# Low halves of the split operands 64 bytes off in SBUF, and the order of three matmuls

## The chip, the core and the metric

The kernel runs on one core of one Trainium2 chip. The metric is the device time of one execution in microseconds (us). Engines are called by the profile's names: PE (TensorE matmul), PEld (TensorE weight load), DVE (VectorE), ACT (ScalarE), POOL (GpSimd) and SP (the queue that issues the DMAs here).

## What is computed

The reference chains three parts over 2 x 576 = 1152 tokens of 512 features:

```python
scores = where(mask, q @ k.T / 8, -1e9); x = softmax(scores) @ v      # 8 heads of 64; a window of 32, or 32 with dilation 4
h = x @ w_in; x = (h * tanh(softplus(h))) @ w_out                     # 512 -> 2048 -> 512, called the first layer here
out = sum_e p[:, e] * (relu(x @ w1[e]) @ w2[e])                       # 4 experts, 512 -> 1024 -> 512, p normalised over e
```

All inputs and outputs are float32.

## The kernel before

**Split operands.** Nearly every large product is made three times. A float32 value is split into a high part (rounded to the type that the kernel calls float32r, by ACT) and a low part (the rest, by DVE or POOL), and a product x·y is taken as high·high + high·low + low·high, three matmuls into one PSUM bank. The tiles come in pairs: `xh`/`xl` (activations), `wxh`/`wxl` (weights of the first layer's units 0 to 3, later other operands), `gh`/`gl` (outputs of the activation function), and `late0`/`late1` and `late2`/`late3` (weights of the other units, later the experts' weights). Each tile is one block per partition; all slices that the matmuls read are whole multiples of 128 bytes long and begin at multiples of 128 bytes inside their tile. Before the change each of these ten tiles begins at a multiple of 128 bytes of its partition: their sizes are multiples of 128 bytes, and the tile `pad` of 48 floats stands behind the three `raw` tiles, `prob` and `psum_e`, whose sizes are not.

**A matmul and its load.** A matmul reads a stationary operand of 128 columns, which a weight load brings into the array, and streams a moving operand of N columns (N is 256, 320 or 512 here, 4 bytes a column and partition) past it. While one matmul streams, the load for the next one runs.

**The four places with split products.** Line 566 (`Step1.first`, x @ w_in), line 590 (`Step1.second`, the activated values @ w_out), line 786 (`Group.prod`, an expert's first products, as seven block products of a Strassen form) and line 861 (`Group.second`, an expert's second products). Their orders of the three matmuls, as (stationary, moving):

- line 566: (w high, x high), (w high, x low), (w low, x high)
- line 590: (w high, g high), (w low, g high), (w high, g low)
- line 786: (a high, b high), (a high, b low), (a low, b high)
- line 861: (g high, w high), (g high, w low), (g low, w high)

**Stages.** Attention runs to about 64 us, with the first steps of the first layer between its pieces. The first layer runs to about 256 us: 48 visits of a unit (16 units for each of three groups of 512, 320 and 320 tokens), each with 12 matmuls of line 566 and 12 of line 590. `steps[i].first()` is issued before `steps[i - 1].second()`, so that ACT and DVE (lines 574 and 575, `split`) make `gh`/`gl` of a step while PE does another. Step 0 takes its low activations last (`lo_last`). Then 4 experts x 2 token sets x 4 pairs of feature blocks run as 32 groups: 42 matmuls of line 786 in each (7 products x 6), and of line 861 24 (set 0, N = 256 in line 786) or 30 (set 1, N = 320). The last group takes its last row in two halves, which makes 6 matmuls more. So there are 576 + 576 + 1344 + 870 = 3366 split matmuls out of 4152; the others belong to attention. Each engine executes in the order written. Nothing waits for an output before the end except the store of the result.

Of the kernel before, what the change touches and what calls it, by code (L numbers as in the profile page):

```python
# [8 lines left out]
F32 = mybir.dt.float32  # L9
F32R = mybir.dt.float32r  # L10
# [13 lines left out]
def kernel(  # L24
# [18 lines left out]
    NT = B * S  # L43
# [3 lines left out]
    NUA = 4  # L47
# [5 lines left out]
    SETS = ((0, 256), (512, 320))  # L53
    GW = 640
    PW = 2816
    EXP, MISH = "exp_and_friends", "mish"

    big = ctx.enter_context(tc.tile_pool(name="big", bufs=1))
# [8 lines left out]
    def bank(n):  # L67
        return ps.tile([128, 512], F32, tag=f"bank{n}", name=nm("bank"))
# [2 lines left out]

    xh = big.tile([128, 4 * NT], F32R, name="xh")
    xl = big.tile([128, 4 * NT], F32R, name="xl")

    wxh = big.tile([128, 1024 * NUA], F32R, name="wxh")
    wxl = big.tile([128, 1024 * NUA], F32R, name="wxl")

    gh = big.tile([128, 2 * GW], F32R, name="gh")  # L80
    gl = big.tile([128, 2 * GW], F32R, name="gl")
    raws = [big.tile([128, 4104], U8, name=f"raw{n}") for n in range(3)]
    prob = big.tile([128, NT // 128, NE], F32, name="prob")
    psum_e = big.tile([128, NT // 128], F32, name="psum_e")
    big.tile([128, 48], F32, name="pad")

    scr = big.tile([128, NT // 128 * DM], F32, name="scr")
    hbuf = [scr[:, GW * n:GW * (n + 1)] for n in (0, 1)]
# [19 lines left out]
    late = []  # L108
# [436 lines left out]
    class Step1:  # L545
# [27 lines left out]
        def split(self):  # L573
            ACT.activation(self.ghi, self.hc, AF.Copy)  # L574
            DVE.tensor_tensor(out=self.glo, in0=self.hc, in1=self.ghi.bitcast(F32), op=ALU.subtract)  # L575

        def second(self, lo_last=False, units_at=(0, 1)):
            if self.grp not in yacc:
                yacc[self.grp] = [bank(b)[:, 0:self.w] for b in ((0, 1, 2, 3), (4, 5, 0, 1), (2, 3, 4, 5))[self.grp]]
            for i, u in enumerate(self.us):  # L580
                if i not in units_at:
                    continue
                wh, wl = units[u]
                g = slice(self.w * i, self.w * (i + 1))
                order = [(d, k) for d in range(4) for k in range(3)]
                if lo_last:
                    order.sort(key=lambda o: o[1] == 2)
                for d, k in order:
                    a, x = ((wh, self.ghi), (wl, self.ghi), (wh, self.glo))[k]
                    PE.matmul(yacc[self.grp][d], a[:, 512 + 128 * d:640 + 128 * d], x[:, g],  # L590
                              start=u == UORD[self.grp][0] and k == 0, stop=u == UORD[self.grp][-1] and k == 2)

# [12 lines left out]
    for n in (0, 1):  # L605
        o = 2 * GW * (n + 1)
# [114 lines left out]
    def prep_a(n):  # L721
        o = PW * (n % NP2)
        r = stage1.rearrange("p (c f m) -> p c f m", c=4, f=2)
        a12 = [w[:, o:o + 512].rearrange("p (c m) -> p c m", c=4) for w in late[2:4]]
        a22 = [w[:, o + 512:o + 768].rearrange("p (c m) -> p c m", c=2) for w in late[2:4]]
        split(*a12, r[:, :, 0], DVE)
        split(*a22, r[:, 2:4, 1], DVE)
        a11, a12, a21, a22 = blocks()
        POOL.tensor_tensor(out=a22, in0=a21, in1=a22, op=ALU.add)  # L729
        POOL.tensor_tensor(out=a21, in0=a11, in1=a21, op=ALU.subtract)  # L730
        POOL.tensor_tensor(out=a11, in0=a22, in1=a11, op=ALU.subtract)
        POOL.tensor_tensor(out=a12, in0=a12, in1=a11, op=ALU.subtract)

    def prep_s(n):
        o = PW * (n % NP2) + 768
        split(late[2][:, o:o + 1024], late[3][:, o:o + 1024], stage1, DVE)
        load_w1(n + 1)
        ready.add(("s", n))

    def w2_hi(n):  # L740
        o = PW * (n % NP2) + 1792
        ACT.activation(late[2][:, o:o + 1024], stage2, AF.Copy)  # L742

    def w2_lo(n):
        o = PW * (n % NP2) + 1792
        hi, lo = (t[:, o:o + 1024] for t in late[2:4])
        POOL.tensor_tensor(out=lo, in0=stage2, in1=hi.bitcast(F32), op=ALU.subtract)  # L747
        load_w2(n + 1)
        ready.add(("w2", n))
# [5 lines left out]
    def amat(name, p, k):  # L755

        o = PW * p
        o += {"A11": 128 * k, "A12": 256 + 128 * k, "A22": 512 + 128 * k, "S2": 768 + 256 * k, "S3": 896 + 256 * k,
# [3 lines left out]
    class Group:  # L762
# [90 lines left out]
        def second(self, f, which=slice(None)):  # L853
            assert ("w2", self.e * NP2 + self.p) in ready
            o = PW * self.p + 1792 + 512 * f
            wh, wl = (w[:, o:o + 512] for w in late[2:4])
# [103 lines left out]
    u1.x_lo()  # L960
    att.close()
    wpb = ctx.enter_context(tc.tile_pool(name="wpb", bufs=1))
    late += [wpb.tile([128, n], F32R, name=f"late{i}") for i, n in enumerate((1024, 1024, 11264, 11264))]
    late.append(wpb.tile([128, 640], F32, name="late4"))


# [28 lines left out]
    for e in range(1, NE):  # L995
        for p in range(NP2):
            n, g = e * NP2 + p, 2 * NP2 * (e - 1) + NP2 + p + 1
# [67 lines left out]
```

## Time and profile before

| | |
|---|---|
| median of 3 runs | 632.99 us (632.98 to 633.09) |
| profiled execution, its own time | 635.62 us |
| its span, first to last instruction | 633.8 us |
| mean granted TensorE clock | 0.997 |
| PE busy | 625.5 us (99%), 4152 matmuls |
| PEld busy | 562.2 us (89%), 4152 loads |
| DVE, ACT, POOL busy | 287.0, 261.9, 180.5 us |

A matmul's recorded duration is longer than the distance to the next one, because matmuls are pipelined. Busy time counts overlapping matmuls once. What a matmul costs in a row of them is the distance from start to start, called the pitch below: the length of a piece in the chain that ended last divided by its count, or the difference of two starts in the timeline.

### The profile page before, as it was taken

How to read it: one execution, taken by the hardware profiler on the slowest of the kernel's cores; microseconds unless marked ns; L12 is line 12 of the kernel's file. 1: busy time of each engine (PE TensorE's matmuls, PEld its weight loads, DVE VectorE, ACT ScalarE, POOL GpSimd, SP SyncE). 2: the span in 40 equal slices, each digit the busy share in tenths (PEclk: the TensorE clock that was granted, in tenths of full speed). 3: DMA queues.
4: the chain of work that ended last, by engine and by line, in shares of the span. 5: the costliest groups of instructions: out<-in, count | busy, mean ns of one | idle time of the engine just before them, and what ended most of it. 6: DMA issues, size and time to landing. Idle time of an engine off the chain costs nothing.

```text
span 633.8 us, 10146 instructions
## 1 busy us (share of the span) xinstructions
PE 625.5 (99%) x4152; PEld 562.2 (89%) x4152; DVE 287.0 (45%) x482; ACT 261.9 (41%) x497; POOL 180.5 (28%) x201
## 2 busy tenths in 40 slices
PE   8998999999999999999999999999999999999997
PEld 5776888889999999998998899998999988989986
DVE  6887677613111333474534523444523444424223
ACT  7786777624223443452344322444322443322220
POOL 8763555512100242180243200234200335100000
PEclk9998999999999999999999999999999999999999
DMA  8865677300000122020023200123100132000102
GB/s 192 195 184 156 222 223 220 128 1 1 1 1 1 67 79 87 1 101 1 13 88 100 66 1 1 34 78 90 67 1 0 34 101 66 2 1 30 38 1 83
DMA packets 51358, 43.66 MB, mean 69 GB/s; under 512 B 26352, under 2 KB 44144, under 8 KB 51312
## 3 DMA queue, kind: packets, MB, share of 16 engines
q1 hardware_dynamic: 51312, 43.02, 22.9%
q8 instruction: 32, 0.52, 0.3%
q14 instruction: 14, 0.11, 0.1%
HBM read 40.65 MB, written 2.36 MB: 68 GB/s over the span
## 4 chain that ended last, share of the span: by engine, by line
PE 92%; DMA 3%; DVE 2%; SPq 1%; ACT 1%; POOL 0%; issue 0%; DVEq 0%; POOLq 0%
PE bank L861 31%; PE bank L786 28%; PE bank L590 16%; PE bank L566 15%; DMA raw<-in_moe_w_out_dram 1%; DMA scr<-in_moe_w_in_dram 1%; DMA vP<-in_v_dram 1%; DMA natk<-in_k_dram 1%; DVE pr L383 1%; DVE mx L382 1%; PE bank L326 0%; SPq L282 0%; PE bank L396 0%; ACT pr L384 0%; PE bank L374 0%; POOL vP L289 0%
## 5 line engine op out<-in xcount | busy, mean ns | idle before, releaser
L786 PE MATMUL bank<-xh,late 128*128 128x256 f32 (+1 forms) x512 | 120.4, 296 | 0.0
L786 PE MATMUL bank<-wxh,late 128*128 128x320 f32 (+1 forms) x384 | 94.9, 296 | 0.0
L786 PEld LDWEIGHTS bank<-xh,late 128*128 128x128 f32 x512 | 89.1, 190 | 1.8
L861 PE MATMUL bank<-late,gh 128*128 128x512 f32 x280 | 87.0, 392 | 0.0
L729 POOL TENSOR_TENSOR raw<-raw 128x256 f32<-128x256 f32 x16 | 12.2, 764 | 225.1 <-DVE late L618 225.1
L566 PE MATMUL bank<-xh,late 128*128 128x320 f32 (+1 forms) x288 | 75.9, 336 | 0.0
L786 PE MATMUL bank<-xl,late 128*128 128x256 f32 (+1 forms) x256 | 75.7, 296 | 0.0
L590 PE MATMUL bank<-gh,late 128*128 128x320 f32 (+1 forms) x288 | 72.0, 336 | 0.0
L786 PEld LDWEIGHTS bank<-wxh,late 128*128 128x128 f32 x384 | 68.5, 190 | 0.6
L575 DVE TENSOR_TENSOR gl<-scr,gh 128x512 fp32r<-128x512 f32 (+1 forms) x32 | 24.5, 767 | 80.0 <-ACT gh L574 80.0
L861 PEld LDWEIGHTS bank<-late,gh 128*128 128x128 f32 x280 | 50.9, 188 | 9.0
L571 ACT ACTIVATE scr<-bank 128x320 f32<-128x320 f32 (+1 forms) x48 | 23.5, 489 | 83.4 <-PE bank L566 83.4
L747 POOL TENSOR_TENSOR late<-raw,late 128x1024 fp32r<-128x1024 f32 x16 | 38.8, 2422 | 64.8 <-ACT late L742 64.8
L786 PE MATMUL bank<-wxl,late 128*128 128x256 f32 (+1 forms) x192 | 56.9, 296 | 0.1
L861 PE MATMUL bank<-late,gl 128*128 128x512 f32 x140 | 54.5, 389 | 0.0
L566 PEld LDWEIGHTS bank<-xh,late 128*128 128x128 f32 x288 | 50.6, 188 | 3.8
L590 PEld LDWEIGHTS bank<-gh,late 128*128 128x128 f32 x288 | 50.1, 188 | 3.7
L861 PE MATMUL bank<-late,late 128*128 128x512 f32 (+1 forms) x219 | 52.8, 388 | 0.0
L786 PEld LDWEIGHTS bank<-xl,late 128*128 128x128 f32 x256 | 48.5, 190 | 1.8
L566 PE MATMUL bank<-xl,late 128*128 128x320 f32 (+1 forms) x144 | 48.3, 336 | 0.0
L590 PE MATMUL bank<-gl,late 128*128 128x320 f32 (+1 forms) x144 | 48.3, 336 | 0.0
L861 PE MATMUL bank<-late,wxh 128*128 128x512 f32 (+1 forms) x154 | 47.4, 389 | 0.0
(153 smaller groups left out, 1137.3 us busy)
## 6 DMA issues: line engine op xcount, KB each, us to landing
raw<-in_moe_w_dram SPq DMA_DIRECT2D x32, 512.0 KB, 3.4
raw<-in_moe_w_out_dram SPq DMA_DIRECT2D x15, 512.0 KB, 3.6
raw<-in_moe_w_in_dram SPq DMA_DIRECT2D x9, 512.0 KB, 4.2
scr<-in_moe_w_in_dram SPq DMA_DIRECT2D x7, 512.0 KB, 4.9
natk<-in_k_dram SPq DMA_DIRECT2D x8, 256.0 KB, 3.5
natq<-in_q_dram SPq DMA_DIRECT2D x8, 256.0 KB, 4.0
out_dram<-scr SPq DMA_DIRECT2D x8, 256.0 KB, 2.0
vD<-in_v_dram SPq DMA_DIRECT2D x16, 64.0 KB, 4.1
```

The lines of the kernel that those rows point to most:

```text
L382: DVE.tensor_reduce(out=mx, in_=sv, axis=AX.X, op=ALU.max)
L383: DVE.tensor_tensor(out=self.pr, in0=sv, in1=mx.unsqueeze(2).to_broadcast([128, 8, 64]), op=ALU.subtract)
L566: PE.matmul(h, a[:, c, :], x[:, c, :], start=c == 0 and k == 0, stop=c == 3 and k == 2)
L571: ACT.activation(self.hc[:, self.w * i:self.w * (i + 1)], h, AF.Mish)
L575: DVE.tensor_tensor(out=self.glo, in0=self.hc, in1=self.ghi.bitcast(F32), op=ALU.subtract)
L590: PE.matmul(yacc[self.grp][d], a[:, 512 + 128 * d:640 + 128 * d], x[:, g], start=u == UORD[self.grp][0] and k == 0, stop=u == UORD[self.gr ...
L729: POOL.tensor_tensor(out=a22, in0=a21, in1=a22, op=ALU.add)
L747: POOL.tensor_tensor(out=lo, in0=stage2, in1=hi.bitcast(F32), op=ALU.subtract)
L786: PE.matmul(out, w, x(k), start=first and k == 0 and i == 0, stop=k == 1 and i == 2, skip_group_check=not first)
L861: PE.matmul(acc, x[:, s], a[:, cols], start=self.p == 0 and f == 0 and i == 0, stop=self.p == NP2 - 1 and f == 1 and i == 2, skip_group_ch ...
```

## The change

The low tiles get 32 floats more, and their slice begins 16 floats (64 bytes) inside; the pad shrinks to 16 floats. In line 590 the second and third matmul change places.

```diff
+    LINE = 16
...
+    def lo_tile(pool, n, name):
+        return pool.tile([128, n + 2 * LINE], F32R, name=name)[:, LINE:LINE + n]
+
     xh = big.tile([128, 4 * NT], F32R, name="xh")
-    xl = big.tile([128, 4 * NT], F32R, name="xl")
+    xl = lo_tile(big, 4 * NT, "xl")
 
     wxh = big.tile([128, 1024 * NUA], F32R, name="wxh")
-    wxl = big.tile([128, 1024 * NUA], F32R, name="wxl")
+    wxl = lo_tile(big, 1024 * NUA, "wxl")
 
     gh = big.tile([128, 2 * GW], F32R, name="gh")
-    gl = big.tile([128, 2 * GW], F32R, name="gl")
+    gl = lo_tile(big, 2 * GW, "gl")
...
-    big.tile([128, 48], F32, name="pad")
+    big.tile([128, 16], F32, name="pad")
...
                 if lo_last:
-                    order.sort(key=lambda o: o[1] == 2)
+                    order.sort(key=lambda o: o[1] == 1)
                 for d, k in order:
-                    a, x = ((wh, self.ghi), (wl, self.ghi), (wh, self.glo))[k]
+                    a, x = ((wh, self.ghi), (wh, self.glo), (wl, self.ghi))[k]
...
-    late += [wpb.tile([128, n], F32R, name=f"late{i}") for i, n in enumerate((1024, 1024, 11264, 11264))]
+    for i, n in ((0, 1024), (2, 4 * PW)):
+        late += [wpb.tile([128, n], F32R, name=f"late{i}"), lo_tile(wpb, n, f"late{i + 1}")]
```

## Rows read from the trace of the kernel before

**Rows 1.** The page, parts 1 and 4: busy time, and the chain that ended last.

```profile
span 633.8 us, 10146 instructions
PE 625.5 (99%) x4152; PEld 562.2 (89%) x4152; DVE 287.0 (45%) x482; ACT 261.9 (41%) x497; POOL 180.5 (28%) x201
...
PE 92%; DMA 3%; DVE 2%; SPq 1%; ACT 1%; POOL 0%; issue 0%; DVEq 0%; POOLq 0%
```

**Rows 2.** Stretches: window in us, PE busy (matmuls), other engines, PEclk, DMA share, GB/s.

```profile
44.00:72.00 28.00, 25.71 (x180) 19.65 (x179) 19.96 (x39) 19.42 (x32) 12.41 (x12) 0.94 0.57 173
72.00:140.00 68.00, 68.00 (x306) 56.62 (x306) 42.47 (x58) 42.79 (x72) 33.31 (x24) 1.00 0.49 155
140.00:250.00 110.00, 110.00 (x746) 109.51 (x745) 30.96 (x41) 39.75 (x71) 19.95 (x18) 1.00 0.09 29
384.00:478.00 94.00, 94.00 (x554) 85.20 (x553) 39.28 (x69) 32.41 (x64) 21.50 (x20) 1.00 0.15 46
```

**Rows 3.** Chain that ended last, in pieces: start us, length us, what, matmuls.

```profile
11.09 0.44 PE bank L326 x4
...
89.21 2.72 PE bank L566 x12
91.93 2.72 PE bank L590 x12
...
147.94 3.52 PE bank L590 x24
151.47 3.52 PE bank L566 x24
...
352.27 4.31 PE bank L786 x36
...
396.19 4.39 PE bank L786 x30
400.58 3.42 PE bank L861 x15
```

**Rows 4.** Timeline at a change from N = 512 to N = 256: start us, length us, instruction.

```profile
340.72 0.39 PE L861 MATMUL bank<-late,gl 128*128 128x512 f32 x1
...
340.95 0.28 PE L786 MATMUL bank<-xh,late 128*128 128x256 f32 x1
340.95 0.19 PEld L786 LDWEIGHTS bank<-xl,late 128*128 128x128 f32 x1
...
341.06 0.28 PE L786 MATMUL bank<-xl,late 128*128 128x256 f32 x1
341.07 0.31 PEld L786 LDWEIGHTS bank<-xh,late 128*128 128x128 f32 x2
...
341.18 0.40 PE L786 MATMUL bank<-xh,late 128*128 128x256 f32 x2
341.30 0.19 PEld L786 LDWEIGHTS bank<-xl,late 128*128 128x128 f32 x1
```

**Rows 5.** Timeline of PE alone at a change from N = 320 to N = 512.

```profile
400.42 0.63 PE L861 MATMUL bank<-late,gh 128*128 128x512 f32 x2
400.89 0.39 PE L861 MATMUL bank<-late,gl 128*128 128x512 f32 x1
401.12 0.63 PE L861 MATMUL bank<-late,gh 128*128 128x512 f32 x2
401.58 0.39 PE L861 MATMUL bank<-late,gl 128*128 128x512 f32 x1
...
402.94 0.39 PE L861 MATMUL bank<-late,gl 128*128 128x512 f32 x1
```

**Rows 6.** Timeline around the second products of one step: the split, then line 590.

```profile
90.12 0.68 DVE L575 TENSOR_TENSOR gl<-scr,gh 128x512 fp32r<-128x512 f32 x1
...
91.77 0.62 PE L590 MATMUL bank<-gh,late 128*128 128x512 f32 x2
...
92.22 0.39 PE L590 MATMUL bank<-gl,late 128*128 128x512 f32 x1
```

**Rows 7.** The end of the kernel in the chain: start us, length us, what.

```profile
619.92 10.31 PE bank L861 x51
630.23 0.03 issue
630.26 0.48 DVE scr L875
```

## The prediction

> **What bounds the kernel.** I read the page's busy times and the chain that ended last first: PE is busy for 625.5 of 633.8 us, and PE makes up 92% of the chain [rows 1]. An average over stages can mislead, so the stretches come next: from 72 us on PE is busy for the whole of each stretch shown, at a granted clock of 1.00, its higher level of 2.4 GHz, while DVE, ACT and POOL are busy for well under two thirds of the same time [rows 2]. So the time is a count of matmuls times their pitch, and only something that changes the pitch can change it. The third view is the chain in pieces, which gives the pitch. Line 590 takes 2.72 us for 12 matmuls of 512 columns, 226.7 ns each, and line 566 the same, although their orders of the three products differ; 24 of 320 columns take 3.52 us, 146.7 ns each, again on both lines; 36 of 256 columns on line 786 take 4.31 us, 119.7 ns each [rows 3]. From 512 to 320 columns the pitch falls by 80.0 ns for 192 columns, 0.4167 ns a column, which is the higher clock. The streams alone then take 213.3, 133.3 and 106.7 ns, and each pitch is 13.3 ns (13.0 for the last) above that. **The gap** is the same for all three sizes and lines, and it is the time in which a stream reads 32 columns, 128 bytes of a partition. 3366 gaps of 13.3 ns are 44.8 us. [...]
>
> **The change, part by part.**
>
> *Offsets.* No instruction is added or removed: 4152 matmuls and as many loads stay. What changes is where a low operand begins: 64 bytes behind a multiple of 128. The high parts keep their place modulo 128: each low tile grows by 128 bytes, and pad goes from 192 to 64 bytes, down by 128. With each tile rounded up to 32 bytes, the three raw tiles (4128 each), prob (160) and psum_e (64) are 12608 bytes; with 64 more that is 99 times 128, as it was 100 times before.
>
> After the change the moving operands of three successive products begin at 0, 64 and 0, and the next triple at 0 again. The loads follow: the load for the next product starts with the running matmul (340.95 and 340.95, 341.06 and 341.07 [rows 4]), and with the new order on line 590 it is always the load of a high part beside a high stream and of a low part beside a low one. Load and stream thus begin at the same place modulo 128 in every pair, as they do before.
>
> No row shows an operand at 64 beside one at 0 in a split product, so the cost of the offset is bounded. [...] Above: where a row of 512 columns follows shorter ones, the first five pitches are 400.42 to 401.58, 232 ns each, and then 401.58 to 402.94, 227 ns each [rows 5]; single ones, from 400.89 to 401.12, are 230. A gap 5.3 ns longer on all would be 17.8 us more; a whole further period of 13.3 ns on the two products in three that have a low operand would be 2244 x 13.3 = 29.9 us more.
>
> I take a value between. The gap equals one period of 128 bytes at three sizes of stream, so I read it as a start that must fall on the same place of a period: a stream of a whole number of periods ends on such a place, is too late for it, and the next start waits a full period. A gap of half that length does occur: when 256 columns follow 512, the first pitch is 0.11 us (340.95 to 341.06) and the next 0.12 [rows 4]; 0.11 leaves about half of the usual gap, though with equal offsets. If a start at 64 has its place half a period later, the gaps from 0 to 64 and from 64 to 0 become 6.67 ns, and the third, from 0 to 0, stays 13.3. That is 2 x 6.67 ns off every three products: 2244 x 6.67 ns = 15.0 us. Some 60 of the products lie before 64 us, between pieces of attention and loads, where PE is idle for part of the time (25.7 us busy of 28.0 from 44 to 72 us [rows 2]); I count their 40 gaps as nothing gained, 0.3 us.
>
> *Line 590's order.* The low activations are read second instead of third, one product (147 to 227 ns) earlier, and the low weights as much later. The split that makes the low activations ends at 90.80 us here, and the first product with them starts at 92.22; in the new order it would at about 92.00 [rows 6]. Of the 32 steps this is the one with the smallest lead, and 1.2 us of it are left. So this costs nothing; without that lead, each of 31 steps (step 0 keeps its low activations last) could lose up to 0.2 us, 7 us in all. For the pitch the order by itself is worth nothing with equal offsets: lines 566 and 590 have the same one [rows 3]. It matters only with the offset, for the pairing above.
>
> *What hides a faster PE's next limit.* The other engines have over a third of each stretch free [rows 2], so they follow a PE that is 2% faster. Behind the last matmul, what remains is 0.5 us of DVE and the store [rows 7], untouched.
>
> *Sum.* The profiled execution takes 635.62 us, 2.63 above the median of 632.99; taking 14.7 us off gives 620.9 for such an execution and 618.3 for the median.
>
> **Rivals.**
>
> *No difference, 633.0.* What sets the gap may be the meeting of the running stream with the load beside it. Both begin together [rows 4] and at the same place modulo 128, before and after, so nothing would change. For it: the gap is the same at all sizes, as one load per matmul would make it. Against it: at 512 columns the load is over long before the stream ends, and the gap is still there. A related rule stands in the Trainium skill, page "TensorE: Matmul & The Clock Gate", section "Step-by-step: what each phase is for": stationary and moving operand have read ports of their own, so a load takes nothing from the running stream, and an offset would not matter. Its section "Back-to-back issue gap" gives N/2.4 + 2.5 ns as the isolated pitch; the trace has 13.3 in place of 2.5 for split products, so there the rule does not describe these rows, and no run here yet shows what an offset does. By that rule the time would be 633.0.
>
> *Slower, 648.0.* If the machine reads whole periods of 128 bytes, a stream that begins at 64 touches one more: 2048 bytes lie in 17 periods instead of 16, 1024 in nine instead of eight. Each product with a low moving operand, one in three, then costs 13.3 ns more: 1122 x 13.3 = 15.0 us, and 648.0. The place is every low stream, and it decides as soon as a partial period costs as much as a whole one. For it: the gap is just one period, as if the machine counted in them. Against it: the short pitch in rows 4 is not a whole number of periods, so a start is not bound to them in every case. The same sum comes out if each change of place costs half a period instead of saving it.
>
> *The offset does not arrive.* If high and low parts moved together, all would stay as it was, at 633.0; the sizes above speak against it, and I give it no chance of its own.
>
> **How the numbers follow.** The half gap on two products in three, or more than that, has 0.53; no difference 0.21; slower 0.26. The likeliest is 618.3. Its own range is 611 (a half gap on all 3366, 22.4 us less) to 626 (on one in three only, 7.5 us less). The range that is to hold 8 times in 10 has to reach over the second case to the third: 606 to 648. It leaves out gaps near 3.3 ns (599) below and the whole further period on two products in three (663) above, some 15 in 100 together with what I have not thought of. A measurement of this kernel can tell about 0.2% from no change, 1.3 us. Faster has 0.53, within 0.2% 0.21, slower 0.26.
>
> **What would show it.** Right: pieces of the chain at 12 matmuls in 2.67 us on lines 566 and 590 instead of 2.72, 24 in 3.41 instead of 3.52, and some 4.15 for 36 on line 786; in the timeline, pitches that alternate by size of gap, shorter around a low stream, and the mean duration of single matmuls a few ns lower. No difference: all pieces as before. Slower: 12 matmuls in 2.77 us or more, with the longer pitch behind the low streams alone if it is the further period. The forecast is wrong if the gap stays 13.3 ns or grows; it is wrong in another way if the pitch falls and idle time of PE with a releaser on DVE or POOL grows instead.

## The result, and the profile after

The changed kernel takes 637.37 us (median of 4 runs, 636.74 to 637.81) against 633.04 for the kernel before on the same chip: a ratio of 1.0060, 95% interval 1.0048 to 1.0073. It is slower by 4.3 us; the forecast was 618.3 and faster.

The page of the profile after, parts 1 and 4:

```profile
span 635.7 us, 10148 instructions
...
PE 628.6 (99%) x4152; PEld 561.6 (88%) x4152; DVE 288.9 (45%) x482; ACT 262.4 (41%) x497; POOL 181.4 (29%) x201
...
PE 96%; DMA 1%; DVE 1%; ACT 1%; SPq 0%; issue 0%; DVEq 0%; ACTq 0%
```

As in [rows 1], the time is PE's: the same 4152 matmuls and loads, and the other engines work about as long as before. The profiled execution took 637.45 us, close to its median.

The stretches of after, in the columns of [rows 2]:

```profile
44.00:72.00 28.00, 27.73 (x196) 21.70 (x194) 23.14 (x44) 22.13 (x38) 14.42 (x14) 1.00 0.63 191
72.00:140.00 68.00, 68.00 (x302) 55.70 (x302) 41.21 (x55) 41.41 (x68) 31.70 (x23) 1.00 0.46 147
140.00:250.00 110.00, 110.00 (x747) 109.48 (x746) 30.97 (x41) 39.43 (x71) 19.91 (x18) 1.00 0.09 29
384.00:478.00 94.00, 94.00 (x549) 84.61 (x548) 39.23 (x69) 32.43 (x64) 21.46 (x20) 1.00 0.15 46
```

The first line shows why the two spans must not be subtracted: in the execution of before the clock was at 0.94 from 44 to 72 us, here it was at 1.00, and PE began 196 matmuls there instead of 180. In the other stretches PE is busy without a break in both kernels and at a granted clock of 1.00 in both. There the same 68 us hold 302 matmuls instead of 306, and the same 94 us hold 549 instead of 554. In the stretch of 320 columns there is no loss (747 against 746). So the pitch has changed, and by how much depends on the shape.

The chain of after, in the columns of [rows 3]:

```profile
87.06 2.79 PE bank L570 x12
...
137.22 3.52 PE bank L570 x24
...
161.18 3.50 PE bank L594 x24
...
352.05 4.27 PE bank L790 x36
356.32 2.80 PE bank L865 x12
...
396.17 4.42 PE bank L790 x30
400.59 3.48 PE bank L865 x15
...
621.61 10.44 PE bank L865 x51
```

Lines 566, 590, 786 and 861 of before are 570, 594, 790 and 865 here. Twelve matmuls of 512 columns in the first layer take 2.79 us instead of 2.72, 232.5 ns each: the gap above the 213.3 ns of streaming is 19.2 ns instead of 13.3. Thirty-six of 256 columns take 4.27 instead of 4.31, a gap of 11.9 ns. At 320 columns the first layer stays within 0.02 us of its 3.52 per 24, and line 790 loses 0.03 per 30.

Summed with the number of products of each shape: 384 of the first layer at 512 columns lose 5.8 ns each (2.2 us); 858 of line 865 at 512 columns lose 3.3 (12 matmuls from 2.75 to mostly 2.79) to 4.0 ns (15 from 3.42 to 3.48), 3.2 us; 672 of line 790 at 320 columns lose 1.0 ns (0.7 us); 672 at 256 columns gain 1.1 ns (0.7 us). That is 5.4 us. The two traces can be compared directly from the first row of 320 columns on, which in before is

```profile
138.17 3.52 PE bank L566 x24
```

From there to the end of the last product before takes 492.06 us (to 630.23 [rows 7]) and after 494.83 (137.22 to 632.05): 2.8 us more, where the sum has 3.2. With the 2.2 us of the first layer's 512 columns that makes 5.0, and the medians say 4.3. The other 0.7 us can come from the part ahead, whose length differs between traces by more than that (see narrow32 below).

The timeline of PE alone in after, to be laid beside [rows 5]:

```profile
100.60 0.40 PE L570 MATMUL bank<-xh,late 128*128 128x512 f32 x1
100.83 0.39 PE L594 MATMUL bank<-gh,late 128*128 128x512 f32 x1
101.07 0.39 PE L594 MATMUL bank<-gl,late 128*128 128x512 f32 x1
101.29 0.63 PE L594 MATMUL bank<-gh,late 128*128 128x512 f32 x2
101.76 0.40 PE L594 MATMUL bank<-gl,late 128*128 128x512 f32 x1
```

Start to start: 230, 240, 220, then two in 470 ns; the five together take 1160 ns, 232 each. The pitch no longer settles to 227 as it does in the second half of [rows 5]; it stays as long as a pitch of the first five there.

### The profile page after: what moved, and what is told of

It reads as the page before. It is cut to its first block, busy times and chain, and to the rows that moved or that the text cites. A ratio compares the mean times of both kernels' runs of the same rounds, so it can differ in the third digit from the quotient of the medians.

```text
span 635.7 us, 10148 instructions
## 1 busy us (share of the span) xinstructions
PE 628.6 (99%) x4152; PEld 561.6 (88%) x4152; DVE 288.9 (45%) x482; ACT 262.4 (41%) x497; POOL 181.4 (29%) x201
## 4 chain that ended last, share of the span: by engine, by line
PE 96%; DMA 1%; DVE 1%; ACT 1%; SPq 0%; issue 0%; DVEq 0%; ACTq 0%
PE bank L865 32%; PE bank L790 28%; PE bank L594 16%; PE bank L570 16%; PE bank L330 1%; DMA natk<-in_k_dram 1%; PE bank L400 1%; PE bank L370 1%; PE bank L378 1%; PE bank L433 1%; DMA natq<-in_q_dram 1%; PE bank L416 0%; PE bank L412 0%; SPq L286 0%; PE bank L365 0%
## 5 line engine op out<-in xcount | busy, mean ns | idle before, releaser
L594 PE MATMUL bank<-gh,late 128*128 128x320 f32 (+1 forms) x288 | 76.4, 338 | 0.0
```

## The experiments

All times are ratios to the kernel before on the same chip, with 95% intervals; a ratio is formed from all runs and need not be the quotient of the two medians. The pieces are given in this order: 12 of 512 columns and 24 of 320 in the first layer, 36 of 256 and 12 of 512 in the experts (these two at about 350 us). Before: 2.72, 3.52, 4.31, 2.75 us. After: 2.79, 3.50 to 3.54, 4.27, 2.80.

### Is it the place, or a difference of places?

**all64** moves every operand, high and low, to 64 bytes:

```diff
+    big.tile([128, 16], F32, name="ahead")
     xh = big.tile([128, 4 * NT], F32R, name="xh")
```

> A tile of 64 bytes ahead of all others moves every operand, high and low, to 64 bytes behind a multiple of 128; all offsets are equal again. If what counts is one operand's place against another's (stream after stream, load after load, or stream beside load), pieces of 12 matmuls of 512 columns stay at 2.72 us and the time at 633.0. If the place 64 costs by itself, the pieces are at 2.79 us or more, as in the changed kernel, and the time is 637 or more.

Measured: 1.0009 [0.9998, 1.0021]; pieces 2.72, 3.52, 4.31, 2.75. The chain:

```profile
86.70 2.72 PE bank L567 x12
...
135.66 3.52 PE bank L567 x24
```

The absolute place costs nothing measurable.

**weights64** leaves high and low parts equal and puts the weights of the later units and experts (`late`) 64 bytes against the activations:

```diff
-    big.tile([128, 48], F32, name="pad")
+    big.tile([128, 32], F32, name="pad")
```

> The pad is 32 floats instead of 48: all weights of units 4 to 15 and all expert weights, high and low, begin at 64, all activations of the first layer at 0. Successive streams keep their place, and so do successive loads. If only a change of place from stream to stream or from load to load counts, the pieces of the first layer stay at 2.72 us (512 columns) and 3.52 us (24 of 320) and the time at 633.0. If the place of the load against that of the stream beside it counts, the pieces change, by 0.05 us or more per 12, and the time moves by 2 us or more, either way.

Measured: 1.0063 [1.0043, 1.0083]. The chain:

```profile
69.71 2.72 PE bank L590 x12
72.43 2.75 PE bank L566 x12
75.18 2.72 PE bank L590 x12
...
352.92 4.24 PE bank L786 x36
357.16 2.80 PE bank L861 x12
```

The same loss in total as the change, with the same sign by shape; in the first layer 12 matmuls of 512 columns lose 0.03 us, less than the 0.05 expected and than the 0.07 of the change, and 320 columns stay at 3.52. The run holds its own comparison: the rows at 69.71 and 75.18 us load weights of `wxh` and `wxl`, which keep their place against the activations, and take 2.72; the row between them loads from `late` and takes 2.75. Within a row from `late` no stream changes place against the one before it, and no load against the load before it: all loads stand 64 bytes from all streams. So a constant difference of load and stream is enough, and a change of place from product to product isn't needed.

### Which part of the change?

**oldorder** is the changed kernel with line 590's old order:

```diff
-                    order.sort(key=lambda o: o[1] == 1)
+                    order.sort(key=lambda o: o[1] == 2)
...
-                    a, x = ((wh, self.ghi), (wh, self.glo), (wl, self.ghi))[k]
+                    a, x = ((wh, self.ghi), (wl, self.ghi), (wh, self.glo))[k]
```

> The changed kernel with the old order on line 590, the offsets kept. If the pairing of load and stream is what the new order serves, the second products of the first layer get slower than in the changed kernel by 0.03 us or more per 12 and the time is 638 or more. If a mix of places is all that counts, the pieces stay within 0.03 us of the changed kernel's (2.79 for 512 columns) and the time within 1 us of 637.4.

Measured: 1.0059 [1.0033, 1.0086]; pieces 2.77 to 2.80, 3.50 to 3.56, 4.26 to 4.28, 2.76 to 2.80. The order is worth nothing measurable, neither for the pitch nor by a wait.

**lowact** and **lowweights** are the kernel before with only the low activations (`xl`, `gl`), or only the low weights (`wxl`, `late1`, `late3`, with the pad of 16), made by the change's `lo_tile`:

```diff
+    def lo_tile(pool, n, name):
+        return pool.tile([128, n + 32], F32R, name=name)[:, 16:16 + n]
+
-    xl = big.tile([128, 4 * NT], F32R, name="xl")
+    xl = lo_tile(big, 4 * NT, "xl")
...
-    gl = big.tile([128, 2 * GW], F32R, name="gl")
+    gl = lo_tile(big, 2 * GW, "gl")
```

> Only xl and gl begin at 64; the order of line 590 is the old one. In the first layer the low streams are off and all loads are at 0. If the change of place from stream to stream is what costs, the 512-column pieces of the first layer are at about 2.79 us on both lines, as in the changed kernel; if it is the change from load to load, they stay at 2.72. Time: 633 to 637, since the expert stage has only part of its low operands moved.

> Only wxl, late1 and late3 begin at 64; the order of line 590 is the old one. In the first layer the low loads are off and all streams are at 0. If the change of place from load to load is what costs, the 512-column pieces of the first layer are at about 2.79 us on both lines; if it is the change from stream to stream, they stay at 2.72 us there, and the cost is only in the expert stage (line 861, where the low streams are late3).

Measured: 1.0051 [1.0034, 1.0068] and 1.0053 [1.0036, 1.0071]; 512-column pieces of 2.77 to 2.79 and 2.76 to 2.81 in the first layer. Each half alone costs about as much as both, so the loss isn't a sum over the products with a low operand. But these two runs changed something else too: a low tile that is 128 bytes longer moves every tile behind it by 128 bytes, which the next runs take apart.

### The period is 256 bytes

**weights128** and **weights256** are weights64 with other pads, so that the late weights stand 128 bytes from the activations, or 256:

```diff
-    big.tile([128, 48], F32, name="pad")
+    big.tile([128, 16], F32, name="pad")
```

in weights128, and 112 in place of the 16 in weights256.

> The pad is 16 floats: all late weights move by 128 bytes against the activations, so they stay equal modulo 128 and differ modulo 256. If only the place modulo 128 counts, pieces of 12 matmuls of 512 columns are at 2.72 us, 36 of 256 at 4.31 us and the time is 633 to 634, as before. If 256 or 512 bytes count, the pieces change as with 64 bytes: 2.75 to 2.80 us, 4.24 us, and 636 to 638.

> The pad is 112 floats: all late weights move by 256 bytes against the activations. If the period is 256 bytes, nothing changes: 2.72 us per 12 of 512 columns, 4.31 per 36 of 256, 633 to 634. If it is 512, the pieces change as they did with 128 bytes: 2.75 to 2.80, 636 to 639.

Measured: 1.0074 [1.0055, 1.0093] and 1.0001 [0.9991, 1.0012]. The chain of weights128, and of weights256:

```profile
88.61 2.79 PE bank L566 x12
...
353.44 4.32 PE bank L786 x36
357.76 2.80 PE bank L861 x12
```

```profile
86.67 2.72 PE bank L566 x12
...
349.73 4.31 PE bank L786 x36
354.05 2.75 PE bank L861 x12
```

Operands that are equal modulo 128 but not modulo 256 are as slow as those at 64; equal modulo 256 they are as fast as before. The "multiples of 128 bytes" by which the kernel before was described misled: there all ten tiles are equal modulo 256 as well, and in the changed kernel they aren't. By their sizes, with the start of `xh` as 0: `wxh` begins at 128 modulo 256 (behind one longer tile), `gh` at 0 (behind two), and `late0` and `late2` are 128 apart.

**mix512** and **after512** split the change along that line. mix512 keeps its longer tiles but lets the low slices begin with their tile:

```diff
-        return pool.tile([128, n + 2 * LINE], F32R, name=name)[:, LINE:LINE + n]
+        return pool.tile([128, n + 2 * LINE], F32R, name=name)[:, 0:n]
```

after512 keeps the 64 bytes but orders the tiles so that all highs are equal modulo 512 and all lows begin 64 bytes later, the late tiles in the same manner:

```diff
     xh = big.tile([128, 4 * NT], F32R, name="xh")
-    xl = lo_tile(big, 4 * NT, "xl")
     wxh = big.tile([128, 1024 * NUA], F32R, name="wxh")
-    wxl = lo_tile(big, 1024 * NUA, "wxl")
     gh = big.tile([128, 2 * GW], F32R, name="gh")
-    gl = lo_tile(big, 2 * GW, "gl")
+    big.tile([128, LINE], F32, name="ahead")
+    xl = big.tile([128, 4 * NT], F32R, name="xl")
+    wxl = big.tile([128, 1024 * NUA], F32R, name="wxl")
+    gl = big.tile([128, 2 * GW], F32R, name="gl")
...
-    big.tile([128, 16], F32, name="pad")
+    big.tile([128, 32], F32, name="pad")
```

> The changed kernel with the low slices at the start of their longer tiles: every operand at 0 modulo 128, and all tiles mixed modulo 512 just as in the changed kernel. If the mix modulo 512 is what costs, it is as slow as the changed kernel: 2.77 to 2.80 us per 12, 636 to 638. If the 64 bytes cost, it is at 2.72 us and 633.

> The changed kernel with its tiles in another order: all high tiles equal modulo 512, all low tiles 64 bytes behind that. In the changed kernel the high tiles were equal modulo 128 only. If it was the new places of the high tiles modulo 512 that cost, the half-period gap may now show: 12 matmuls of 512 columns at 2.72 us or less (2.67 as forecast), 618 to 633 us. If the 64 bytes themselves unsettle the row, it stays at 2.75 to 2.80 us and 636 to 638.

Measured: 1.0064 [1.0043, 1.0085] and 1.0067 [1.0044, 1.0089]. The chain of mix512, and of after512:

```profile
86.97 2.79 PE bank L570 x12
...
351.61 4.29 PE bank L790 x36
355.89 2.78 PE bank L865 x12
```

```profile
89.32 2.77 PE bank L592 x12
...
157.10 3.57 PE bank L568 x24
...
352.64 4.23 PE bank L788 x36
356.87 2.77 PE bank L863 x12
```

Either alone makes the whole loss: 128 bytes of mixing without any low part at 64, and clean 64 bytes without any mixing. In after512 the load of a high part runs beside a high stream and that of a low part beside a low one, as the prediction wanted it, and the pitch is long all the same; there even 320 columns lose (3.57).

**lowact256** and **lowweights256** repeat the two halves with tiles 256 bytes longer, so that nothing but the named low parts changes place modulo 256:

```diff
+        return pool.tile([128, n + 64], F32R, name=name)[:, 16:16 + n]
```

> Only the two low activation tiles begin 64 bytes off; they grow by 256 bytes, so that every other tile keeps its place modulo 256, and the order of line 590's counterpart is the old one. In the first layer every weight load is then at one place, and only the succession of moving streams changes place (one product in three). If the change of place from stream to stream, or of a stream against the load beside it, unsettles the pitch, 12 matmuls of 512 columns in the first layer take 2.75 us or more and the total is 635 to 637. If only the loads' succession counts, the first layer stays at 2.72 and 3.52, only the experts change (there the activations are stationary in the second products), and the total is 633 to 635. If the whole loss of the earlier run with the low activations came from its 128-byte mixing, nothing changes: 633.0.

> Only the three low weight tiles begin 64 bytes off; they grow by 256 bytes, so that all else keeps its place modulo 256, old order. In the first layer every moving stream is then at one place, and only the succession of weight loads changes place. If load against stream, or load after load, unsettles the pitch, 12 of 512 columns in the first layer take 2.75 us or more and the total is 635 to 637. If only streams count, the first layer stays at 2.72 and only the experts' products change, where low weights are the moving operand. If only the 128-byte mixing counted, nothing changes: 633.0.

Measured: 1.0019 [1.0007, 1.0031] and 1.0035 [1.0023, 1.0047]. The chain of lowact256 and of lowweights256:

```profile
89.06 2.80 PE bank L569 x12
91.86 2.78 PE bank L593 x12
...
156.03 3.47 PE bank L593 x24
```

```profile
87.53 2.77 PE bank L569 x12
...
154.33 3.52 PE bank L593 x24
```

In the first layer of lowact256 all loads are at one place and one stream in three is moved; in that of lowweights256 all streams are at one place and one load in three is moved. Both lengthen the pitch at 512 columns. What the two have in common, with each other and with weights64, is a stationary and a moving operand that differ modulo 256 bytes. The third expectation, that it was all the mixing, falls. The total of lowact256 (634.8 us) stays under the 635 to 637 expected. New here: with the low streams moved alone, 24 matmuls of **320** columns take 3.47 to 3.48 us instead of 3.52, a gap of some 11.4 ns; over the 768 products of 320 columns in the first layer that gives back some 1.5 us of the loss at 512.

### Other distances

**weights32**, **weights96** and **plus32** are weights64 with pads of 24, 40 and 56 floats: with the places taken modulo 256, the late weights begin 96 or 32 bytes earlier, or 32 later, than the activations.

> The late weights begin 32 bytes behind a multiple of 128, the activations of the first layer at 0. If any unequal place unsettles the row of matmuls, 12 matmuls of 512 columns take 2.74 to 2.80 us and 36 of 256 columns 4.22 to 4.28 us. If it is the half of the period alone, they stay at 2.72 and 4.31.

> As before with 96 bytes. If any unequal place unsettles the row of matmuls, 2.74 to 2.80 us and 4.22 to 4.28 us; if the half of the period alone does, 2.72 and 4.31. A difference between 32 and 96 would say that it matters which of load and stream is ahead.

> The late weights 32 bytes ahead of the activations' place modulo 512 instead of 32 behind. If the sign does not matter, 12 of 512 columns take 2.80 us and 36 of 256 take 4.20, as with 32 behind; if it does, the 256-column pieces differ by 0.05 us or more.

Measured: 1.0104 [1.0075, 1.0133], 1.0067 [1.0048, 1.0085] and 1.0079 [1.0052, 1.0107]. At 512 columns every distance gives 2.80 in the first layer; at 320 columns each gives 3.52. At 256 columns they differ: 4.32, 4.20 and 4.26; the 4.20 of weights96 lies outside both of its expected lengths. The chain of weights96, and of plus32:

```profile
88.59 2.80 PE bank L566 x12
...
353.38 4.20 PE bank L786 x36
357.59 2.81 PE bank L861 x12
```

```profile
353.56 4.26 PE bank L786 x36
```

So the sign of the difference matters at 256 columns. The rows of 512 columns are shortest with equal places, those of 256 aren't: there a load 32 bytes earlier than the stream takes 3.1 ns off each matmul.

### A version that beats both

**narrow32** gives that distance to the products of 256 columns alone. The tiles `xh`, `xl`, `wxh`, `wxl` get 56 floats ahead, from where set 0's operands are read and written, and so 32 bytes later modulo 256 than their loads; spacers and another order of the tiles keep all else equal modulo 256:

```diff
+    def wide(n, name, skip):
...
+        t = big.tile([128, 56 + n], F32R, name=name)
+        return t, t[:, 56:]
...
+    xh0, xh = wide(4 * NT, "xh", False)
...
-            bm[0].setdefault(name, []).append(two(h, 512 * m, n0, n0))
+            bm[0].setdefault(name, []).append(two(h0, 512 * m, n0, n0))
```

> The kernel before, with set 0's moving operands of the products of 256 columns read 32 bytes ahead of their stationary operands modulo 256, and all other operands equal modulo 256. If a shorter gap belongs to the rows in which load and stream differ, 36 matmuls of 256 columns take 4.20 us instead of 4.31, the pieces of 512 and 320 columns stay at 2.72 and 3.52, and the total falls by about 672 x 2.9 ns = 1.9 us to 631.0. If the unsettling carries over into the following rows of 512 columns, line 861's counterpart rises to 2.80 per 12 and the total is 632 to 634. If the shorter gap needed 512-column rows to be unequal as well, 256 columns stay at 4.31 and the total is 633.

Measured: 0.9986 [0.9974, 0.9999]. The chain:

```profile
88.48 2.72 PE bank L571 x12
...
137.44 3.52 PE bank L571 x24
...
350.95 4.20 PE bank L791 x36
355.15 2.75 PE bank L866 x12
...
617.21 10.31 PE bank L866 x51
```

The pieces are as the first expectation has them: 4.20, and the rows of 512 behind them keep 2.75. The total fell by 0.9 us (0.1 to 1.6 by the interval) to a median of 632.85, less than the 2.0 us that 672 products times 3.1 ns make. In the trace these 2.0 us are there in full: from the first row of 320 columns to the end of the last product narrow32 takes 490.08 us (137.44 to 627.52) against 492.06 in before, 2.0 less. So part of the saving goes in the part ahead. It ends at 137.44 us here, at 135.66 in the trace of all64, whose pieces are as long as those of before, and at 138.17 in that of before, with its clock of 0.94 from 44 to 72 us; why it is longer here than in all64, no run shows.

**narrow_both** adds to it what lowact256 showed: in the first layer's groups of 320 columns the low activations and low activated values begin 64 bytes later. For room, `xh` and `xl` are cut into a tile for the first group and set 0, and one for the rest, and the tiles are ordered anew:

```diff
+    xhb = big.tile([128, XB], F32R, name="xhb")
+    xha = big.tile([128, XA + 8], F32R, name="xha")
+    xla = big.tile([128, XA + 8], F32R, name="xla")
+    xlb = big.tile([128, 16 + XB], F32R, name="xlb")
...
-        return t[:, 4 * c:4 * (c + n)].rearrange("p (s n) -> p s n", s=4)
+        o = 4 * c - (XA if g else 0) + (16 if g and t is xl else 0)
+        return t[1 if g else 0][:, o:o + 4 * n].rearrange("p (s n) -> p s n", s=4)
...
-            self.ghi, self.glo = gh[:, g], gl[:, g]
+            self.ghi, self.glo = gh[:, g], gl[:, 16 if grp else 0:][:, g]
...
+    xh0, xl0 = xha[:, 8:], xla[:, 8:]
```

> As narrow32 (set 0's moving operands of 256 columns 32 bytes ahead of their loads), and in the first layer's two groups of 320 columns the low activations and low activated values stand 64 bytes behind the rest; all other operands equal modulo 256. If the rows' lengths go by the places of their own operands alone and add up, 36 matmuls of 256 columns take 4.20 us, 24 of 320 in the first layer take 3.47 instead of 3.52, pieces of 512 columns stay at 2.72, and against the kernel before 2.0 + 1.5 us go: a ratio of 0.9945, some 629.6 us. If the shorter pitch at 320 columns came from what stood before it in lowact256 (unequal rows of 512), 3.52 stays and the ratio is that of narrow32, 0.9986.

Measured: medians of 630.69 us against 633.74, and a ratio of 0.9963 [0.9949, 0.9978], where 0.9945 was expected. The chain:

```profile
89.89 2.72 PE bank L598 x12
...
136.13 3.54 PE bank L574 x24
...
152.89 3.47 PE bank L598 x24
...
348.31 4.20 PE bank L795 x36
...
614.57 10.31 PE bank L870 x51
```

Each row has the length that its own operands' places gave it in the other runs, whatever ran before it. From the first row of 320 columns to the end of the last product the trace takes 488.75 us (136.13 to 624.88), 3.3 less than before, so the two savings add up there (1.3 us more than narrow32's 2.0). The total is faster than both kernels; by the ratio it is 2.3 us under the kernel before (1.4 to 3.2). The pieces alone (672 x 3.1 ns + 768 x 1.9 ns) make 3.5, a little more than the interval allows.

## Why the prediction was wrong

**What bounds the kernel** held. The time is a count of matmuls times their pitch [rows 1 to 3]; the change altered the pitch and nothing else, and PE stayed busy throughout.

**The step that failed** is the reading of the gap: "I read it as a start that must fall on the same place of a period", from which followed gaps of 6.67 ns beside a low operand. There is no such saving: in the first layer of the changed kernel the gap is 19.2 ns at 512 columns. No piece shown of any run has a mean gap under 10 ns, and at 512 columns, where the forecast had 2.67 us for 12, every difference of places tried in the first layer lengthened it, to between 2.75 and 2.80 in the pieces shown. weights64 and all64 show why the picture was wrong: with high and low equal and the weights moved as a whole, no start changes place from one stream to the next, and the pitch is long; with everything moved together it is as before. What counts at 512 columns is not where a start falls but whether stationary and moving operands fall together. The short first pitch in [rows 4], from which I took "a gap of half that length does occur", is one pitch at a change of shape, read off starts given to 10 ns; it was too thin to carry 15 us. Nor is the gap the same on all lines: [rows 3] has 15 matmuls of line 861 in 3.42 us, a gap of 14.7 ns, though all operands are equal there.

**"The high parts keep their place modulo 128"** was true and not enough. That 128 was the period came from the gap's length alone (the time of 32 columns). weights128 against weights256 shows 256. The change therefore did more than its diff says: its 128 bytes of growth per low tile moved the highs against one another, and mix512 shows that this by itself costs all of it.

**The bounds.** No run shows a gap near the 3.3 ns that the range left out below; the least mean of a piece shown is 10.0. The bound above that was taken from [rows 5], a gap 5.3 ns longer, came out about right in size for one shape: at 512 columns the gap grew by 5.8 ns in the first layer and 3.3 to 4.0 in line 865. In part that is luck, for in [rows 5] all operands are equal, and no run shows that its first pitches and those of the changed kernel have one cause. And I applied it to all 3366 products (17.8 us); it holds for the 1242 of 512 columns, while those of 320 lose 1.0 ns or nothing and those of 256 go the other way.

**The rivals.** "No difference" was right that the place of a stationary operand against a moving one matters, and wrong that pairing load and running stream by the order keeps the time: after512 has just that pairing and loses 0.67%. The rule weighed there, from the Trainium skill, page "TensorE: Matmul & The Clock Gate", section "Step-by-step: what each phase is for", that a load takes nothing from the running stream because each has a read port of its own, is not enough to describe these rows. In the first layer of lowweights256 no stream moves, only a third of the loads by 64 bytes, and 12 matmuls take 2.77 us instead of 2.72; whether the load takes anything from the running stream there, no run shows. "Slower, 648.0" had the sign by a wrong mechanism: a further period per low stream is refuted by all64, where every operand begins 64 bytes off and the pieces keep their lengths, and by weights64, where no low part stands apart and the loss is the same.

**Order and cover.** The order of line 590 was put at nothing, and oldorder confirms it (1.0059 against the change's 1.0060); its shorter lead for the low activations cost nothing measurable either.

**Not settled.** Why a difference lengthens the pitch at 512 columns, leaves 320 mostly alone and shortens 256, no run shows; nor which stationary operand is the partner that counts: after512 shows that an equal pair of running stream and load beside it isn't enough to keep 2.72. In every longer row of the first layer shown, some products' own two operands differ, which makes that pair the simplest candidate, but a kernel in which a product's own two operands are equal and its neighbours' differ wasn't tried.

## What to carry to other kernels

Where a stream of split float32r matmuls bounds a kernel, try stationary and moving operands at the same place modulo 256 bytes when they stream 512 columns (in the first layer here 2.72 us per 12, against 2.75 to 2.80), and check the addresses of all tiles after any change of a tile's size: a tile that grows by 128 bytes moves its neighbours. A narrower stream may have another best distance (here the load 32 bytes earlier than the stream at 256 columns, low streams 64 bytes off at 320), and it is found by reading the piece of the chain for that shape, not the total. Before a pattern in the gaps is turned into a mechanism, ask which pairs of operands are equal in the kernel at hand, since a trace in which all are equal cannot say what a difference does.

## What the runs showed of the hardware that was not expected

- With all operands equal modulo 256 bytes the gap between matmuls is 13.3 ns at 512 and 320 columns in the first layer, 13.0 at 256, and 14.7 to 15.8 at 512 columns on line 861. With a stationary operand elsewhere than the moving one it is 15.8 to 20 ns at 512 columns in the first layer (2.75 to 2.80 us for 12), and between 10.0 and 13.3 at 256 (4.20 to 4.32 for 36).
- The period of the effect is 256 bytes: 128 apart costs 0.74% of the kernel, 256 apart nothing measurable.
- One stream in three out of place costs a row of 512 columns no less than every load out of place: 12 take 2.78 to 2.80 us in lowact256, 2.75 in weights64 and 2.80 in weights96.
- The gap can be shortened by placement alone, to 10.0 ns at 256 columns and 11.4 at 320, and in narrow_both the shapes don't disturb one another.
